# Attention and two MLPs in one program: far weights' conversions counted as ready later, block copies urgent, the first load's gate due sooner

## The chip, the cores and the metric

The kernel runs on one core of a Trainium2 chip. The metric is the device time of one execution in microseconds (us). TensorE multiplies, VectorE, ScalarE and GpSimd do everything between the products, and SyncE (SP) issues all loads and stores. In rows of the profile these are PE (and PEld for its weight loads), DVE, ACT, POOL and SP.

## What is computed

```python
# q, k, v: (2, 8, 576, 64) float32
q_rot, k_rot = rotate(q), rotate(k)                    # rotary positions
scores = q_rot @ k_rot.T / 8
scores = scores - max(scores)
attn = exp(scores); attn = attn / (attn.sum() + 1e-9)
x = attn @ v                                           # -> (1152, 512)
h = maximum(x @ w_in, 0.0)                             # w_in (512, 2048)
y = (h * h) @ w_out                                    # w_out (2048, 512)
out = ((y @ w_a) * (y @ w_b)) @ w2_out                 # (512, 1536) twice, (1536, 512)
```

## The kernel before

**The parts.** The attention part works on eight pairs of heads. A pair has five chunks of scores, (p, 0) to (p, 4), the last a small one. VectorE takes the maximum of a chunk while it moves it out of PSUM (line 440), ScalarE takes the exponent (445), VectorE transposes (462), and TensorE multiplies with V (498), one pair behind. GpSimd rotates q and k of the pair after next (364, 365). Sums of a pair become reciprocals (`recip`, 526: a bias on ScalarE, the reciprocal on VectorE, then `pieces` on GpSimd, which cuts them into three bf16 parts), TensorE turns these (`flip`, 545) and spreads them over the rows (`spread`, 560), and GpSimd scales x (`scale`, 583).

The first MLP has 16 slices of 128 columns. The first four are computed plainly (`unit1`), the others two by two in super blocks (`super1`), and `out1` multiplies with `w_out` in four groups. The second MLP has 12 super blocks (`super2`) for each half of the tokens and sums with `w2_out` (`out2`). A super block makes seven products p1 to p7 of half size instead of eight, with sums and differences of the operands. It keeps partial results in three PSUM banks: after p1, p7 and p6 a copy by ScalarE saves the bank's content (lines 912, 916, 920 in `super2`, 961, 965, 969 in `super1`), and the next product into the same bank is added on top, so p6 waits for p1's copy, p4 for p7's and p5 for p6's.

**Conversion of weights.** The weights arrive as 64-bit floats, 512 KB a slice, and are turned into two float32r parts. `convert` (612) issues the load, then ScalarE scales (622), GpSimd or VectorE clamps (631), VectorE shifts (625) and merges the bits (628). `two_parts` (608) makes the high half on ScalarE and the low half, value less high half, on VectorE or GpSimd (606). For super blocks `prep_pair` adds four sums and differences (689 and after). There are three buffers for raw slices, two each for the scaled ones and for the bits.

**The planner.** The whole order is fixed when the program is built. Each piece of work is an `Op` with the engines that may do it, a cost, its inputs and its buffers. TensorE's order is that in which the ops are written; `order` gives the others a due time, backward from the TensorE op that needs them (`soon` and `anchor` can pull it ahead: due so many us behind the anchor's due time). Then it plays the program through: at each step it takes, over all engines, the op that can start first. On one engine, of the ops that can start first the one due first wins, and only an `urgent` op may be preferred when it can start up to `WAIT` = 0.3 us later. `FLEX` ops, open to VectorE and GpSimd, go to whichever can start them first. The times in the plan are the planner's own; on the chip an engine keeps the planned order and starts each op when its inputs are there.

**Gates and pacing.** Three one-element memsets (1077) stand behind chunks (0, 4), (6, 1) and (6, 3): the loads of the first, second and third weight wait for one each in the plan, later ones for all. `paced` holds the first two weights' scaling back until the exponents of (6, 2) and (7, 2).

Of the kernel before, what the change touches and what calls it, by code (L numbers as in the profile page):

```python
# [74 lines left out]
class Plan:  # L75
# [9 lines left out]

    def op(self, engines, cost, fn, after=(), acq=(), rel=()):
        o = Op((engines,) if isinstance(engines, str) else engines or ("-",), cost, fn, after, acq, rel, len(self.ops))
        self.ops.append(o)
        return o

# [19 lines left out]
        return 0.25 + 2.05 * n  # L110

    RATE = 0.33

    def lasts(self, o, e, s, other):
        took = self.takes(e, o.cost)
# [4 lines left out]
    def order(self):  # L120
# [73 lines left out]
        while True:  # L194
# [5 lines left out]
            for e in engines[1:]:  # L200
                ok = []
                for o in open_[e]:
                    if o.end is None and (r := room(o)) is not None:
                        ok.append((max(at[e], begin(o, e), r), o.due, o.k, o, e))
                first = None
                if ok:
                    near = min(x[0] for x in ok) + self.NEAR
                    x = min((x for x in ok if x[0] <= near + self.WAIT * x[3].urgent), key=lambda x: (0 if e == "SP" else x[1], x[0], x[2]))
                    first = (x[0], x[1], x[3], e)
                if first and (best is None or first[0] < best[0]):  # L210
                    best = first
# [39 lines left out]
def attention_moe_moe2_kernel(ctx: ExitStack, tc: tile.TileContext, qk, rope, vq, ident_in, sel_in, w_in, w_out, w_a, w_b, w2_out, out):  # L251
# [274 lines left out]
    def recip(p):  # L526
        st = ST[p]
        rest = lazy(lambda: st_p.tile([P, 9], F32, tag="rest", name=f"rest{p}"))
        part = lazy(lambda: st_p.tile([P, 27], BF16, tag="part", name=f"part{p}"))
        ex = [x for c in range(5) for x in EXP[p, c][1]]  # L530
        def pieces(e):
            e.tensor_copy(part()[:, 0:9], st()[:, 1, :])
            e.tensor_tensor(out=rest(), in0=st()[:, 1, :], in1=part()[:, 0:9], op=ALU.subtract)
            e.tensor_copy(part()[:, 9:18], rest())
            e.tensor_tensor(out=part()[:, 18:27], in0=rest(), in1=part()[:, 9:18], op=ALU.subtract)

        o = pl.op("ACT", ("us", 0.2), lambda e: e.activation(st()[:, 1, :], st()[:, 1, :], AF.Copy, bias=1e-9), ex)
        o = pl.op("DVE", ("us", 0.14), lambda e: e.reciprocal(st()[:, 1, :], st()[:, 1, :]), [o])
        o = pl.op("POOL", ("us", 1.0), pieces, [o])
        SC[p] = o, part  # L540

    def flip(p, slots, at):
# [108 lines left out]
    count = [0]  # L651
# [7 lines left out]
    def prep_weight(key):  # L659
        if key in W:  # L660
            return
        name = f"{key[0]}{key[1]}"
        b = Buf("bits", tile_of([P, DM], I32, "bits", f"bits_{name}", bufs=2))
        w = slot(name)
        early = count[0] <= EARLY
        o = convert(key, Bits(b), early, count[0] <= MID)
        W[key] = w
        WOK[key] = two_parts(name, DM, lambda: w()[:, 0], lambda: w()[:, 1], lambda: b().bitcast(F32), [o], [b], "POOL" if early else FLEX)
        WOK[key][0].acq.append(w)

    ORDER = {1: (0, 0), 2: (0, 1), 7: (1, 0), 4: (1, 1), 5: (2, 0), 6: (2, 1), 3: (3, 0)}

    def prep_pair(key, ka, kb):
# [2 lines left out]
            return  # L676
        ba = Buf("bits", tile_of([P, DM], I32, "bits", f"bits_p{f}", bufs=2))
        bb = Buf("sums", tile_of([P, 6, 256], I32, "sums", f"sums_{f}"))
        oa = convert(ka, Bits(ba), False)
        ob = convert(kb, Bits(bb, 2), False)  # L680
        w = [slot(f"p{f}_{i}") for i in range(4)]
# [16 lines left out]
        for k, (n, after) in enumerate(((2, [s3, ob]), (2, [s1, s2]), (1, [s4]))):  # L698
# [2 lines left out]
            r[0].acq.append(t)  # L701
            ends += r
        pl.op(None, None, None, ends + [s1, s2, s3, s4], rel=[bb])
        W[key], WOK[key] = w, ok + ends

    def use(key, op):
# [189 lines left out]
    def super2(f, t):  # L896
# [12 lines left out]
        def p1():  # L909
            prep_pair(key, ("a", f), ("b", f))  # L910
            o = prod("al", 1)
            op[1] = pl.op("ACT", ("p", HB), lambda e: e.copy(left(), bk["al"]()), [o], acq=[v])  # L912

        def p7():
            o = prod("be", 7)
            op[7] = pl.op("ACT", ("p", HB), lambda e: e.copy(right(), bk["be"]()), [o, op[1]])

        def p6():
            o = prod("al", 6, [op[1]])
            op[6] = pl.op("ACT", ("p", HB), lambda e: e.copy(u(), bk["al"]()), [o], acq=[u])  # L920

        def p2():
            o = prod("gm", 2)
# [20 lines left out]
    def super1(r, t):  # L944
# [13 lines left out]
        def p1():  # L958
            prep_pair(key, ("i", 2 * r), ("i", 2 * r + 1))
            o = prod("al", 1)  # L960
            op[1] = pl.op("ACT", ("p", HB), lambda e: e.copy(v()[:, lo], bk["al"]()), [o], acq=[v])

        def p7():
            o = prod("be", 7)
            op[7] = pl.op("ACT", ("p", HB), lambda e: e.copy(u()[:, hi], bk["be"]()), [o, op[1]], acq=[u])

        def p6():
            o = prod("al", 6, [op[1]])
            op[6] = pl.op("ACT", ("p", HB), lambda e: e.copy(u()[:, lo], bk["al"]()), [o, op[7]])  # L969

        def p2():
            o = prod("gm", 2)
# [93 lines left out]
    for n, (p, c) in enumerate(order):  # L1066
# [8 lines left out]
        if (p, c) in GATES:  # L1075
            k = GATES.index((p, c))
            wide.append(pl.op("DVE", ("us", 0.06), lambda e, k=k: e.memset(sb.tile([P, DM], I64, tag="raw", bufs=3, name=f"later{k}").bitcast(I32)[:, 0:1], 0), EXP[p, c][1]))
    p = NPAIR - 1
    lasts = [SDONE[6, 4]] + TOK[7]
    pl.op(None, None, None, lasts, rel=[held("g2"), held("g3")])  # L1080
# [150 lines left out]
```

## Time and profile before

| | us |
|---|---|
| median of three runs | 540.14 |
| lowest and highest of them | 538.04, 542.59 |
| the profiled execution | 539.17 |
| its span, first to last instruction | 537.4 |
| TensorE busy in it | 525.0 (98%) |
| VectorE, GpSimd, ScalarE busy | 450.5, 358.0, 306.7 |
| TensorE's granted clock, share of full | 0.999 |

The span is what the rows of the trace lie in; the execution is 1.8 us longer. A busy share is an average over stages, so what a stage can give is read from its own windows and from what TensorE waits for in it. Attention ends near 122 us, the first MLP near 325 us.

### The profile page before, as it was taken

Reading aid. Unit: us, or ns where it says so; the run is one execution under the profiler, and the core shown is the slowest. Engines: PE = TensorE matmul, PEld = TensorE weight load, DVE = VectorE, ACT = ScalarE, POOL = GpSimd, SP = SyncE. Lnnn points to the kernel's source line nnn. Section 1 sums busy time; section 2 is a strip of 40 time slices with the busy share of each in tenths; the row PEclk is TensorE's granted clock in tenths of the full one; section 3 lists DMA queues with packets and bytes.
Section 4 is the critical chain, followed back from the end, with each engine's and each line's share of the span. In section 5 each row is a group of like instructions: output and inputs, shape, how many; then the busy total and the mean of one; then the engine's idle time right before and its main releaser. Section 6 shows DMA issues by size and latency. Waiting matters only on the chain.

```text
span 537.4 us, 13363 instructions
## 1 busy us (share of the span) xinstructions
PE 525.0 (98%) x5390; PEld 473.2 (88%) x5390; DVE 450.5 (84%) x809; ACT 306.7 (57%) x756; POOL 358.0 (67%) x297
## 2 busy tenths in 40 slices
PE   8999999999999899999999998999999999999997
PEld 6666666668999899999999998999999999999996
DVE  5998898897899989889978999898778888788454
ACT  1666888887776685378348645557534444443210
POOL 3875789857899458658636899985578776854000
PEclk9999999999999999999999999999999999999999
DMA  7678777464313413322333202333233223300004
GB/s 231 177 179 179 177 179 183 129 187 142 115 48 114 157 47 112 118 80 79 98 113 105 72 9 78 118 117 121 89 108 113 84 79 117 119 1 0 1 2 176
DMA packets 18914, 58.48 MB, mean 109 GB/s; under 512 B 2313, under 2 KB 4489, under 8 KB 17828
## 3 DMA queue, kind: packets, MB, share of 16 engines
q1 hardware_dynamic: 18852, 57.63, 35.8%
q8 instruction: 42, 0.69, 0.6%
q14 instruction: 20, 0.16, 0.1%
HBM read 55.26 MB, written 2.36 MB: 107 GB/s over the span
## 4 chain that ended last, share of the span: by engine, by line
PE 88%; DVE 7%; issue 1%; DMA 1%; ACT 1%; SPq 0%; POOL 0%; DVEq 0%
PE m L711 13%; PE m L713 13%; PE m L712 13%; PE s L412 8%; PE av L498 8%; PE av L711 6%; PE av L713 6%; PE av L712 6%; PE m L1023 3%; PE m L1024 3%; PE m L1025 3%; PE av L1023 2%; PE av L1024 2%; PE av L1025 2%; PE s L408 1%
## 5 line engine op out<-in xcount | busy, mean ns | idle before, releaser
L445 ACT ACTIVATE PV<-PV,st 128x576 f32<-128x576 f32 x48 | 37.0, 771 | 24.1 <-DVE PV L440 23.7
L364 POOL TENSOR_TENSOR X<-X,cs_rot 128x1152 f32<-128x1152 f32 x14 | 36.9, 2642 | 14.1 <-DMA X<-in_qk 14.0
L440 DVE TENSOR_SCALAR_CACHE_REDUCE PV<-s 128x576 f32<-128x576 f32 x48 | 34.4, 753 | 11.5 <-PE s L412 11.5
L606 POOL TENSOR_TENSOR g<-v,g 128x576 fp32r<-128x576 f32 (+1 forms) x23 | 28.7, 1247 | 20.4 <-ACT g L728 20.4
L631 POOL TENSOR_SCALAR cl_i<-cl_i 128x512 f32<-128x512 f32 x15 | 29.4, 1965 | 7.5 <-ACT cl_i L622 6.5
L713 PE MATMUL m<-g,w_o 128*128 128x384 f32 (+1 forms) x99 | 31.9, 322 | 0.0
L712 PE MATMUL m<-g,w_o 128*128 128x384 f32 (+1 forms) x99 | 31.9, 322 | 0.0
L711 PE MATMUL m<-g,w_o 128*128 128x384 f32 (+1 forms) x99 | 31.9, 322 | 0.0
L728 ACT CAST g<-v 128x576 fp32r<-128x576 f32 (+1 forms) x36 | 21.3, 593 | 18.1 <-DVE v L939 16.7
L764 DVE TENSOR_TENSOR oacc<-m,oacc 128x512 f32<-128x512 f32 (+1 forms) x30 | 20.4, 680 | 13.3 <-PE m L1025 13.1
L498 PE MATMUL av<-PT_acc,PV 32*64 32x160 f32 (+1 forms) x1152 | 25.7, 294 | 2.0 <-issue 2.0
L498 PEld LDWEIGHTS av<-PT_acc,PV 32*64 32x64 f32 x1152 | 19.8, 130 | 7.9 <-issue 6.3
L711 PE MATMUL m<-x,w_b 128*128 128x288 f32 x84 | 24.8, 295 | 1.6 <-ACT v L969 1.6
L412 PE MATMUL s<-cs_rot 64*128 64x288 f32 x128 | 24.4, 434 | 1.4 <-DVE PV L440 0.7
L412 PE MATMUL s<-rot 64*128 64x288 f32 x128 | 24.7, 433 | 1.0 <-DVE bits_i L628 0.7
L498 PE MATMUL av<-PT_wb,PV 32*64 32x160 f32 (+1 forms) x1152 | 25.6, 294 | 0.0
L498 PEld LDWEIGHTS av<-PT_wb,PV 32*64 32x64 f32 x1152 | 19.7, 130 | 6.3 <-issue 4.8
L713 PE MATMUL m<-x,w_b 128*128 128x288 f32 x84 | 24.8, 295 | 0.0
L712 PE MATMUL m<-x,w_b 128*128 128x288 f32 x84 | 24.8, 295 | 0.0
L912 ACT COPY v<-m 128x288 f32<-128x288 f32 x16 | 6.4, 400 | 31.6 <-PE m L713 31.6
L713 PE MATMUL m<-x,w_pp 128*128 128x288 f32 x78 | 23.0, 295 | 0.0
L712 PE MATMUL m<-x,w_pp 128*128 128x288 f32 x78 | 23.0, 295 | 0.0
(324 smaller groups left out, 2156.9 us busy)
## 6 DMA issues: line engine op xcount, KB each, us to landing
PV<-in_vq SPq DMA_DIRECT2D x32, 288.0 KB, 4.5
raw_i<-in_w_in SPq DMA_DIRECT2D x16, 512.0 KB, 3.8
raw_o<-in_w_out SPq DMA_DIRECT2D x16, 512.0 KB, 4.1
X<-in_qk SPq DMA_DIRECT2D x26, 288.0 KB, 5.2
raw_a<-in_w_a SPq DMA_DIRECT2D x12, 512.0 KB, 3.8
raw_b<-in_w_b SPq DMA_DIRECT2D x12, 512.0 KB, 3.7
raw<-in_w_out SPq DMA_DIRECT2D x12, 512.0 KB, 3.7
out<-oacc SPq DMA_DIRECT2D x8, 256.0 KB, 2.0
```

What stands on the lines that cost most here:

```text
L364: m = pl.op(where, ("s", 2 * S), lambda e, qi=qi: e.tensor_tensor(out=x()[:, :, qi, :], in0=x()[:, :, qi, :], in1=cs, op=ALU.mult), [done[ ...
L412: pe.matmul(s[h]()[:, bk, 0:288], q0, k0[h][:, bk * 288:bk * 288 + 288], start=True, stop=True)
L440: m = pl.op("DVE", ("us", 0.7), lambda e, h=h, j=j: e.tensor_scalar(out=PP[pr.k][:, h, :].rearrange("p (b n) -> p b n", b=2), in0=s[h]()[: ...
L445: x = pl.op("ACT", ("us", 0.8), lambda e, h=h, j=j: e.activation(PP[pr.k][:, h, :], PP[pr.k][:, h, :], AF.Exp, bias=st()[:, 0, j:j + 1], s ...
L498: pe.matmul(AV[a]()[half(h), q], v[r, h, b], pt[r, k:k + 4 + both, 32 * b:32 * b + 32], start=(b == 0), stop=(b == KB - 1), skip_group_che ...
L606: e.tensor_tensor(out=out_, in0=a, in1=b, op=ALU.subtract)
L631: e.tensor_scalar(out=dst(), in0=cl(), scalar1=-HI * TURN, scalar2=HI, op0=ALU.max, op1=ALU.min)
L711: pe.matmul(dst, wh, mh, start=first, stop=False, skip_group_check=open_)
L712: pe.matmul(dst, wh, ml, start=False, stop=False, skip_group_check=open_)
L713: pe.matmul(dst, wl, mh, start=False, stop=last, skip_group_check=open_)
L1023: pe.matmul(b(), gt[:, 0, c], w[:, 0, d], start=(k == 0), stop=False)
L1024: pe.matmul(b(), gt[:, 0, c], w[:, 1, d], start=False, stop=False)
```

## The change

Ops made while `pl.far` is set are marked far: those of single weights from the ninth slot on, and all of the pairs. In the choice of the next op, a far op on ScalarE or VectorE that is due more than `AWAY` = 6 us behind its inputs counts as able to start 0.8 us later than its inputs allow (`MARGIN`); an op whose engine or buffer is free later than that is not touched. On GpSimd nothing is added. The six copies behind p1, p7 and p6 become urgent. The pieces of the reciprocals are due 4 us behind their pair's last chunk, the gates' memsets 2.5 us behind their chunk.

```diff
--- before.py
+++ after.py
@@ -85,6 +85,7 @@
 
     def op(self, engines, cost, fn, after=(), acq=(), rel=()):
         o = Op((engines,) if isinstance(engines, str) else engines or ("-",), cost, fn, after, acq, rel, len(self.ops))
+        o.far = self.far
         self.ops.append(o)
         return o
 
@@ -110,6 +111,7 @@
         return 0.25 + 2.05 * n
 
     RATE = 0.33
+    MARGIN, AWAY, far = {"ACT": 0.8, "DVE": 0.8}, 6, False
 
     def lasts(self, o, e, s, other):
         took = self.takes(e, o.cost)
@@ -201,7 +203,8 @@
                 ok = []
                 for o in open_[e]:
                     if o.end is None and (r := room(o)) is not None:
-                        ok.append((max(at[e], begin(o, e), r), o.due, o.k, o, e))
+                        b = begin(o, e)
+                        ok.append((max(at[e], b + (self.MARGIN.get(e, 0) if o.far and o.due > b + self.AWAY else 0), r), o.due, o.k, o, e))
                 first = None
                 if ok:
                     near = min(x[0] for x in ok) + self.NEAR
@@ -537,6 +540,7 @@
         o = pl.op("ACT", ("us", 0.2), lambda e: e.activation(st()[:, 1, :], st()[:, 1, :], AF.Copy, bias=1e-9), ex)
         o = pl.op("DVE", ("us", 0.14), lambda e: e.reciprocal(st()[:, 1, :], st()[:, 1, :]), [o])
         o = pl.op("POOL", ("us", 1.0), pieces, [o])
+        o.soon, o.anchor = 4.0, SDONE[p, 4]
         SC[p] = o, part
 
     def flip(p, slots, at):
@@ -663,10 +667,12 @@
         b = Buf("bits", tile_of([P, DM], I32, "bits", f"bits_{name}", bufs=2))
         w = slot(name)
         early = count[0] <= EARLY
+        pl.far = count[0] > 8
         o = convert(key, Bits(b), early, count[0] <= MID)
         W[key] = w
         WOK[key] = two_parts(name, DM, lambda: w()[:, 0], lambda: w()[:, 1], lambda: b().bitcast(F32), [o], [b], "POOL" if early else FLEX)
         WOK[key][0].acq.append(w)
+        pl.far = False
 
     ORDER = {1: (0, 0), 2: (0, 1), 7: (1, 0), 4: (1, 1), 5: (2, 0), 6: (2, 1), 3: (3, 0)}
 
@@ -676,6 +682,7 @@
             return
         ba = Buf("bits", tile_of([P, DM], I32, "bits", f"bits_p{f}", bufs=2))
         bb = Buf("sums", tile_of([P, 6, 256], I32, "sums", f"sums_{f}"))
+        pl.far = True
         oa = convert(ka, Bits(ba), False)
         ob = convert(kb, Bits(bb, 2), False)
         w = [slot(f"p{f}_{i}") for i in range(4)]
@@ -701,6 +708,7 @@
             r[0].acq.append(t)
             ends += r
         pl.op(None, None, None, ends + [s1, s2, s3, s4], rel=[bb])
+        pl.far = False
         W[key], WOK[key] = w, ok + ends
 
     def use(key, op):
@@ -910,14 +918,17 @@
             prep_pair(key, ("a", f), ("b", f))
             o = prod("al", 1)
             op[1] = pl.op("ACT", ("p", HB), lambda e: e.copy(left(), bk["al"]()), [o], acq=[v])
+            op[1].urgent = True
 
         def p7():
             o = prod("be", 7)
             op[7] = pl.op("ACT", ("p", HB), lambda e: e.copy(right(), bk["be"]()), [o, op[1]])
+            op[7].urgent = True
 
         def p6():
             o = prod("al", 6, [op[1]])
             op[6] = pl.op("ACT", ("p", HB), lambda e: e.copy(u(), bk["al"]()), [o], acq=[u])
+            op[6].urgent = True
 
         def p2():
             o = prod("gm", 2)
@@ -959,14 +970,17 @@
             prep_pair(key, ("i", 2 * r), ("i", 2 * r + 1))
             o = prod("al", 1)
             op[1] = pl.op("ACT", ("p", HB), lambda e: e.copy(v()[:, lo], bk["al"]()), [o], acq=[v])
+            op[1].urgent = True
 
         def p7():
             o = prod("be", 7)
             op[7] = pl.op("ACT", ("p", HB), lambda e: e.copy(u()[:, hi], bk["be"]()), [o, op[1]], acq=[u])
+            op[7].urgent = True
 
         def p6():
             o = prod("al", 6, [op[1]])
             op[6] = pl.op("ACT", ("p", HB), lambda e: e.copy(u()[:, lo], bk["al"]()), [o, op[7]])
+            op[6].urgent = True
 
         def p2():
             o = prod("gm", 2)
@@ -1075,6 +1089,7 @@
         if (p, c) in GATES:
             k = GATES.index((p, c))
             wide.append(pl.op("DVE", ("us", 0.06), lambda e, k=k: e.memset(sb.tile([P, DM], I64, tag="raw", bufs=3, name=f"later{k}").bitcast(I32)[:, 0:1], 0), EXP[p, c][1]))
+            wide[-1].soon, wide[-1].anchor = 2.5, SDONE[p, c]
     p = NPAIR - 1
     lasts = [SDONE[6, 4]] + TOK[7]
     pl.op(None, None, None, lasts, rel=[held("g2"), held("g3")])
```

## Rows read from the trace of the kernel before

**Rows 1.** The page's head and part 1: busy us (share of the span) xinstructions.

```profile
span 537.4 us, 13363 instructions
...
PE 525.0 (98%) x5390; PEld 473.2 (88%) x5390; DVE 450.5 (84%) x809; ACT 306.7 (57%) x756; POOL 358.0 (67%) x297
```

**Rows 2.** Windows: stretch and length, each engine's busy us, clock, DMA share, GB/s.

```profile
29.00:36.00 7.00, 6.73 (x197) 4.78 (x197) 6.85 (x14) 4.61 (x13) 3.60 (x7) 1.00 0.92 228
185.30:303.00 117.70, 117.70 (x799) 117.68 (x800) 101.38 (x204) 74.19 (x180) 75.81 (x63) 1.00 0.28 90
303.00:326.70 23.70, 22.32 (x169) 22.09 (x167) 23.06 (x35) 10.99 (x20) 22.14 (x15) 1.00 0.20 65
326.70:332.20 5.50, 5.04 (x37) 4.81 (x37) 5.47 (x8) 4.76 (x12) 5.50 (x5) 1.00 0.28 105
332.20:516.00 183.80, 183.80 (x1192) 172.47 (x1193) 148.96 (x260) 84.91 (x176) 117.23 (x89) 1.00 0.25 78
```

**Rows 3.** TensorE's waits: line, releaser, us in total, times, longest.

```profile
PE m L711 <- ACT v L969: 1.6, 1, 1.6
PE av L711 <- ACT v L912: 1.4, 1, 1.4
...
PE r L545 <- POOL part L535: 0.5, 2, 0.3
```

**Rows 4.** Timeline near 183 us: start, us, what [idle before <-releaser].

```profile
182.62 0.29 PE L713 MATMUL m<-parts,w_b 128*128 128x288 f32 x1
...
184.28 0.62 ACT L609 CAST w_o<-bits_o 128x512 fp32r<-128x512 f32 x1 [2.38 <-DVE bits_o L628]
...
184.81 0.39 ACT L969 COPY v<-m 128x288 f32<-128x288 f32 x1
...
185.25 0.41 PE L711 MATMUL m<-x,w_b 128*128 128x288 f32 x1 [1.55 <-ACT v L969]
```

**Rows 5.** Timeline near 325 us.

```profile
324.24 0.30 PE L713 MATMUL av<-x,w_b 128*128 128x288 f32 x1
...
325.08 0.62 ACT L609 CAST w_pp<-bits_pp 128x512 fp32r<-128x512 f32 x1 [2.80 <-DVE bits_pp L628]
...
326.32 0.39 ACT L912 COPY v<-av 128x288 f32<-128x288 f32 x1
...
326.77 0.40 PE L711 MATMUL av<-parts,w_b 128*128 128x288 f32 x1 [1.44 <-ACT v L912]
```

**Rows 6.** Timeline near 332 us.

```profile
331.68 0.45 DVE L935 TENSOR_TENSOR v<-av,v 128x288 f32<-128x288 f32 x1
...
332.18 0.40 PE L711 MATMUL av<-x,w_b 128*128 128x288 f32 x1 [0.39 <-DVE v L935]
```

**Rows 7.** Line 606: VectorE's ns min/median/max; GpSimd's busy us, mean ns.

```profile
L606 DVE TENSOR_TENSOR w_pp<-sums_p,w_pp x12: 681/1068/1919, 310.0 to 492.2; 128x512 fp32r<-128x512 f32 x8, 128x256 fp32r<-128x256 f32 x4
...
L606 POOL TENSOR_TENSOR w_pp<-sums_p,w_pp 128x512 fp32r<-128x512 f32 x8 | 11.4, 1419 | 5.4 <-ACT w_pp L609 4.4 <-PE av L713 1.0
```

**Rows 8.** Timeline near 34 us.

```profile
33.14 0.21 DVE L538 RECIPROCAL st<-st 128x9 f32<-128x9 f32 x1
...
34.57 0.23 PE L545 MATMUL r<-small,part 128*27 128x128 bf16 x1 [0.27 <-POOL part L535]
```

**Rows 9.** Timelines of GpSimd, TensorE and SP: a rotation, loads, and their uses.

```profile
29.09 1.42 POOL L365 TENSOR_TENSOR cs_rot<-X 128x576 f32<-128x576 f32 x1
...
35.75 0.51 PE L412 MATMUL s<-cs_rot 64*128 64x288 f32 x2
...
90.34 0.42 SPq L620 DMA_DIRECT2D raw_i<-in_w_in  x1
...
104.50 0.31 SPq L478 DMA_DIRECT2D PV<-in_vq  x1
...
110.55 0.69 PE L498 MATMUL av<-PT_wb,PV 32*64 32x160 f32 x28
```

**Rows 10.** Part 6 of the page: V loads, KB each, median us to landing.

```profile
PV<-in_vq SPq DMA_DIRECT2D x32, 288.0 KB, 4.5
```

## The prediction

> **What bounds the kernel now.** The first view to read is the page's busy times. TensorE is busy 525.0 us of a span of 537.4 us, 98% [rows 1], and the windows of the two long quiet stretches, 185.3 to 303 us and 332.2 to 516 us, have it busy for all of their 117.70 and 183.80 us [rows 2]. VectorE, ScalarE and GpSimd have room in both. So an edit can win only where TensorE stands still, and that is 537.4 - 525.0 = 12.4 us in all, the wait for the first inputs and the last output among it.
>
> The second view is TensorE's list of waits, which says where [rows 3]. Three entries touch this change: 1.6 us, once, for a ScalarE copy at line 969; 1.4 us, once, for the ScalarE copy at line 912; and 0.5 us, in two waits, for GpSimd's pieces of the reciprocals (line 535).
>
> The third view is the timeline around the two large ones, where the reader is to see one pattern twice. In the first [rows 4], TensorE wants the copy that starts at 184.81 us (p6 of a block of the first MLP). The product that it copies ended near 182.9 (the matmul of 182.62 is its last), and ScalarE had been idle from 181.90. But next in ScalarE's order stood the high half of a far weight, `w_o<-bits_o`, and that waited 2.38 us for VectorE's merge. TensorE lost 1.55 us, and 0.41 - 0.29 = 0.12 more in its first matmul behind the stop: 1.67 us. In the second [rows 5], p1's product ended near 324.5 us, ScalarE stood idle for 2.80 us in front of a high half that waited for a merge (325.08), and only behind it came the copy that TensorE wanted (326.32): 1.44 + 0.40 - 0.29 = 1.55 us. Both times the planner had believed the conversion to be ready sooner than it was.
>
> **The change part by part.** Four edits, all to the order that the planner writes; no instruction is added or taken away.
>
> *Ready 0.8 us later, and urgent copies.* In the plan, a far weight's operation on ScalarE or VectorE now counts as ready 0.8 us after its inputs if it is due over 6 us later, and a block's copies p1, p7 and p6 may be preferred when they become ready up to 0.3 us after another candidate. Together, a copy that the plan has ready up to 1.1 us after the high half now goes ahead of it. At 183 us the merge really ended near 184.2, some 1.3 us after the copy could have run. In the plan it came before the copy, by an amount that no trace shows. But ScalarE was free only from 181.90, so a merge planned between 181.8 and the copy's 182.9 is overtaken; I take it that this holds. The copy (0.39 us) then ends near 183.3, before TensorE's stop begins at 185.25 - 1.55 = 183.70, and 1.67 us go. Bounds: 0 if the plan had the merge still earlier, 1.67 if not. The 117.70 us behind have no idle time of TensorE [rows 2], so nothing there takes the gain back. The high half behind the copy comes 0.4 us later, and by the edit's own condition it has over 6 us.
>
> At 325 us the copy may go first in the same way, and 1.55 us go there. What is late next is VectorE: from 326.70 to 332.20 us it is busy 5.47 of 5.50 us [rows 2], and its addition at line 935, which TensorE waits for until 332.18 anyhow, stands in that queue at 331.68 [rows 6]. TensorE that comes 1.55 us sooner waits 1.55 us longer. Bounds: 0 (all given back) to 1.55 + 0.39 + 0.40 - 0.29 = 2.05 us (VectorE's queue gets shorter as well). I take 0.3 us, near the lower end: VectorE's idle time in the 23.70 us before is 23.70 - 23.06 = 0.64 us [rows 2], and half of that could close.
>
> The condition also moves work. GpSimd's candidates are not counted later, so an operation that either engine may do now goes to GpSimd when that one is free within 0.8 us. A low half of 512 columns takes 1.42 us there on average; on VectorE the low halves of that tile take 0.68 us at best and 1.92 at worst [rows 7]. From 332.2 to 516 us GpSimd has 183.80 - 117.23 = 66.6 us to spare [rows 2], so there I take 0; where it has none is a rival below.
>
> VectorE's spread for one kind of operation has a rule beside it. The Trainium skill (Trainium Architecture — The Big Picture, "What this means for kernel authors") says that VectorE and GpSimd contend for a shared port pair by an exclusive lock and not by a split of bandwidth. By that rule work handed to GpSimd would give VectorE nothing back while it runs; the 0.3 us at 325 would be 0 and the whole sum 2.2 us. The spread, a factor of 2.8, agrees with it, though no row shows what GpSimd held at the time.
>
> *Pieces of the reciprocals.* They, and through the planner's backward pass the reciprocal and the bias before them, are now due 4 us after their pair's last score. Before, the first pair's reciprocal ran at 33.14 us, and TensorE's transpose waited for the pieces until 34.57 [rows 8]. One reciprocal of 0.21 us per pair moves ahead of VectorE's transposes, and four small GpSimd operations ahead of a rotation. Gain 0.5 us [rows 3], bounds 0 to 0.5.
>
> *The gates' memsets.* The first one lets the first weight's load go; with a due time 2.5 us behind its scores it moves to the end of the first pair, and the load, whose buffer is still fresh then, goes out there and not at 90.34 us [rows 9]. That is 512 KB more just ahead of the stretch of 29 to 36 us, where the DMA engines are 0.92 busy at 228 GB/s [rows 2]: 2.3 us for what is queued behind it on SP, the V loads and the planes of q and k of the pairs after. Cover: the third pair's rotation ends at 29.09 + 1.42 = 30.51 and TensorE uses it at 35.75, 5.2 us later [rows 9]. Cost 0, and up to 2.3 us if that cover is gone. The conversion itself is held back by pacing until pair 6, so this wins nothing either. The second and third weight's loads move up too, ahead of pair 6's last V loads. Of these the last leaves at 104.50, lands 4.5 us later in the median, at 109.0, and is used at 110.55 [rows 9, 10]: a cover of 1.5 us against 2.3 us, at most 0.8 us lost. I take 0, since the loads would have to meet exactly.
>
> Sum: 1.67 + 0.3 + 0.5 = 2.5 us.
>
> **The rivals.**
>
> *Both stalls stay gone (faster than forecast).* VectorE's stretch from 303 to 332 us gets lighter by two or three operations of 0.68 us that go to GpSimd. For it: VectorE is what TensorE waits for there. Against it: GpSimd is itself busy 22.14 of 23.70 us [rows 2]. It gives 1.67 + 2.05 + 0.5 = 4.2 us.
>
> *The edits change the order but not the end.* The merges were planned over 1.1 us ahead of the copies, or what is won comes back as a wait for the next VectorE operation. The pieces' 0.5 us or nothing is left. For it: the merge was late by some 1.3 us, more than the 0.8 that is added, so all depends on where the plan had the copies.
>
> *GpSimd becomes the bound (slower).* Between 303 and 332 us the new count hands GpSimd far low halves ahead of the splits that the second MLP's products need. Each costs 1.42 us, and GpSimd has 23.70 - 22.14 = 1.56 us left: from the second one on, each delays the splits by 1.42 us. The 2.5 us are gone with (2.5 + 1.56) / 1.42 = 2.9, so three of them; 5.4 us above the time before takes (5.4 + 2.5 + 1.56) / 1.42 = 6.7, seven. For it: GpSimd has hardly any idle time there, and none at all from 326.70 to 332.20 us [rows 2]. Against it: an engine so busy is seldom free within 0.8 us, and then the plan hands it nothing more.
>
> **How the numbers follow.** The profiled execution took 539.17 us for its span of 537.4; the 1.8 us around it stay. 539.17 - 2.5 = 536.7. The median of the three runs, 540.14, lies 0.97 above this execution, so I add that: 537.6 us. Chances: the forecast 0.45 (by itself 536 to 539); both stalls gone 0.22 (540.14 - 4.2 = 535.9); no effect 0.19 (539.6 to 540.1); GpSimd the bound 0.14 (from 540 upward, with half of it above 542). The three runs lie within 4.55 us of each other, so a median of such runs may be off by about a third of that, 1.5 us: 535.9 - 1.5 = 534.4 and 540.1 + 1.5 = 541.6 bound the range, with about a tenth left out on either side. A difference of 1%, 5.4 us, is about what a measurement of this kernel can tell from no change. A gain of that size needs the first rival and a low draw on top, or a wait gone that I have not counted: 0.11. A loss of that size needs seven misplaced operations, half of the last rival: 0.08. Within 1%: 0.81.
>
> **What would show it.** Right: no wait for lines 969 and 912 in TensorE's list, the copy ahead of the high half on ScalarE in both places, a wait for line 935 of about 2 us near 329, the pieces' wait gone, the first weight's load before 30 us and no longer wait for rotations. Wrong: a wait for line 969 of the old size (the plan's lead was larger), TensorE held by a split from GpSimd near 325 us (the slower rival), no wait for line 935 (the first rival), or new waits for V loads near 110 us.

## The result and the profile after

The changed kernel takes 535.12 us in the median of eight runs (533.13 to 538.5), against 540.24 us of eight runs of the kernel before on the same chip: a ratio of 0.9899, with a 95% interval of 0.9875 to 0.9924. The medians lie 5.1 us apart, and the ratio amounts to 5.5 us. The forecast of 537.6 us lay on the right side and the time lies in the range of 534.4 to 541.6, but twice the 2.5 us came. At 1.0% it stands on the bound between faster and same, with a chance of 0.11 given to the one and 0.81 to the other.

The page after the change, whose first lines answer to [rows 1] (busy us, share of the span):

```profile
span 533.4 us, 13367 instructions
...
PE 524.1 (98%) x5390; PEld 473.1 (89%) x5390; DVE 421.1 (79%) x768; ACT 305.1 (57%) x756; POOL 397.4 (74%) x338
```

The span is 4.0 us shorter, as is the profiled execution (539.17 to 535.20 us), with TensorE still at 98%. VectorE went from 450.5 to 421.1 us and GpSimd from 358.0 to 397.4: work did move there as the prediction read it from the missing margin. TensorE's list of waits, the same view as [rows 3]:

```profile
PE av L501 <- issue: 1.2, 1, 1.2
PE av L390 <- POOL small L1077: 1.0, 1, 1.0
PE m L719 <- DVE v L946: 0.9, 1, 0.9
PE s L415 <- DVE cs_rot L379: 0.8, 1, 0.8
PE s L415 <- DVE PV L443: 0.8, 1, 0.8
PE m L719 <- ACT v L925: 0.8, 1, 0.8
PE s L415 <- DVE bits_i L632: 0.7, 1, 0.7
```

Code lines have moved: p1's, p7's and p6's copies are now lines 920, 925 and 930 in the second MLP and 972, 977 and 982 in the first, p5's addition is 946 (it was 935), the reciprocals' last piece 538. The waits for the pieces, for p6's copy and for p1's copy are gone. New are 0.8 us for p7's copy (925), and the wait for p5's addition has grown from 0.4 to 0.9 us.

TensorE runs the same instructions in the same order in both kernels, so each can be compared with itself. The table says how far it comes sooner, worked out from the two traces. A stop without releaser is one for which the profile shows no engine and no load that ended it (`issue` in the list above).

| instruction at, before (us) | sooner by (us) | what lies just ahead of it |
|---|---|---|
| 39.75 | 0.27 | first wait for the pieces is gone |
| 50.11 | 1.51 | a stop without releaser at 48.8 is gone |
| 55.75 | 1.79 | small shifts between |
| 90.75 | 0.23 | a stop without releaser has come at 89.0 (after) |
| 97.50 | 1.49 | the one at 96.2 is gone |
| 104.55 | 1.83 | second wait for the pieces is gone |
| 109.39 | 2.13 | shorter wait for a score eviction |
| 185.25 | 3.81 | p6's copy is no longer waited for |
| 326.77 | 5.39 | p1's copy is no longer waited for |
| 328.46 | 4.54 | p7's copy is |
| 332.18 | 3.87 | p5's addition is |
| the end | 3.97 | |

In the steps of the prediction: pieces 0.27 + 0.34 = 0.6 us (0.5 forecast), p6 1.68 us (1.67), p1's stop 1.58 us won and 0.85 + 0.67 us given back, so 0.06 net (0.3). These are 2.3 us. What the sum did not have is 1.2 us of stops without a releaser and small shifts between them (1.24 + 0.28 - 1.56 + 1.26), and 0.3 us at a score eviction.

The two places in the timeline, columns as in [rows 4] and [rows 5]. ScalarE and TensorE near 181 us after the change:

```profile
179.37 0.62 ACT L613 CAST w_o<-bits_o 128x512 fp32r<-128x512 f32 x1 [0.49 <-DVE bits_o L632]
...
180.85 0.40 ACT L982 COPY v<-m 128x288 f32<-128x288 f32 x1
...
181.44 0.29 PE L719 MATMUL m<-x,w_b 128*128 128x288 f32 x1
...
191.47 0.62 ACT L613 CAST w_o<-bits_o 128x512 fp32r<-128x512 f32 x1
```

The high half at 179.37 is not the one of [rows 4]: it is the one ahead of it, which ran at 180.97 us before. The one that held up p6's copy (184.28 before, the third of its kind from 170 us on in both traces) now runs at 191.47 us, 10 us behind the copy and without a wait, and TensorE goes on at 181.44 with no wait. ScalarE, VectorE and TensorE between 320 and 329 us:

```profile
320.85 0.40 ACT L920 COPY v<-m 128x288 f32<-128x288 f32 x1 [3.79 <-PE m L721]
...
322.41 0.45 DVE L772 TENSOR_TENSOR yacc<-av,yacc 128x288 f32<-128x288 f32 x1
...
322.86 0.29 PE L721 MATMUL av<-x,w_pp 128*128 128x288 f32 x1
322.89 0.67 ACT L613 CAST x<-yacc 128x576 fp32r<-128x576 f32 x1 [1.64 <-DVE yacc L772]
323.47 0.39 ACT L925 COPY v<-m 128x288 f32<-128x288 f32 x1
...
323.92 0.40 PE L719 MATMUL m<-parts,w_b 128*128 128x288 f32 x1 [0.76 <-ACT v L925]
...
326.26 1.62 DVE L610 TENSOR_TENSOR gT<-yacc,gT 128x576 f32<-128x576 f32 x1
...
327.81 0.44 DVE L946 TENSOR_TENSOR v<-m,v 128x288 f32<-128x288 f32 x1
...
328.30 0.40 PE L719 MATMUL m<-x,w_b 128*128 128x288 f32 x1 [0.95 <-DVE v L946]
```

p1's copy (320.85) now runs as soon as its product is done. But the next thing on ScalarE is the high half of a split of y (322.89), which waited 1.64 us for VectorE's late eviction of 322.41, and p7's copy stands behind that. It is the old pattern with another op: the splits are not far, so neither edit touches it. The other half is the one that was forecast: p5's addition at 327.81 stands behind a difference of 1.62 us that VectorE began at 326.26; the one of [rows 6] stood behind a difference of 1.62 us too, begun at 330.13. The windows of the stretch, columns as in [rows 2]:

```profile
181.00:299.00 118.00, 118.00 (x803) 117.84 (x802) 93.42 (x195) 74.04 (x182) 86.88 (x75) 1.00 0.29 94
299.00:322.70 23.70, 23.70 (x181) 23.70 (x180) 22.54 (x33) 9.55 (x17) 21.94 (x15) 1.00 0.13 45
322.70:328.20 5.50, 3.90 (x28) 3.43 (x26) 4.96 (x7) 4.23 (x9) 5.50 (x4) 1.00 0.29 95
```

TensorE now stands still in none of the 23.70 us ahead of 322.7, and for 5.50 - 3.90 = 1.6 us of the 5.50 behind, where it stood 0.46 of 5.50 us before. From 181 to 299 us nothing stops it, as forecast.

### The profile page after: what moved, and what is told of

It reads as the page before. It is cut to its first block, busy times and chain, and to the rows that moved or that the text cites. A ratio compares the mean times of both kernels' runs of the same rounds, so it can differ in the third digit from the quotient of the medians.

```text
span 533.4 us, 13367 instructions
## 1 busy us (share of the span) xinstructions
PE 524.1 (98%) x5390; PEld 473.1 (89%) x5390; DVE 421.1 (79%) x768; ACT 305.1 (57%) x756; POOL 397.4 (74%) x338
## 4 chain that ended last, share of the span: by engine, by line
PE 91%; POOL 3%; DVE 2%; issue 1%; DMA 1%; ACT 0%; SPq 0%; DVEq 0%
PE m L719 13%; PE m L721 13%; PE m L720 13%; PE av L501 9%; PE s L415 8%; PE av L721 6%; PE av L719 6%; PE av L720 6%; PE m L1037 3%; PE m L1038 3%; PE m L1039 3%; PE s L411 2%; PE av L1037 1%; PE av L1038 1%; PE av L1039 1%
## 5 line engine op out<-in xcount | busy, mean ns | idle before, releaser
L610 POOL TENSOR_TENSOR g<-v,g 128x576 fp32r<-128x576 f32 (+1 forms) x26 | 32.0, 1230 | 34.1 <-ACT g L736 34.1
L920 ACT COPY v<-m 128x288 f32<-128x288 f32 x20 | 8.0, 398 | 39.2 <-PE m L721 39.2
L635 POOL TENSOR_SCALAR cl_i<-cl_i 128x512 f32<-128x512 f32 x14 | 27.2, 1949 | 2.1 <-ACT cl_i L626 2.1
L720 PE MATMUL m<-x,w_pp 128*128 128x288 f32 x92 | 27.2, 295 | 0.0
L721 PE MATMUL m<-x,w_pp 128*128 128x288 f32 x92 | 27.2, 295 | 0.0
L719 PE MATMUL m<-x,w_pp 128*128 128x288 f32 x92 | 27.1, 294 | 0.0
L719 PE MATMUL m<-x,w_b 128*128 128x288 f32 x82 | 24.3, 296 | 0.9 <-DVE v L946 0.9
L1037 PE MATMUL m<-w_b,g 128*128 128x512 f32 (+1 forms) x63 | 24.6, 390 | 0.0
```

Of the source, the lines that this page charges most:

```text
L610: e.tensor_tensor(out=out_, in0=a, in1=b, op=ALU.subtract)
L635: e.tensor_scalar(out=dst(), in0=cl(), scalar1=-HI * TURN, scalar2=HI, op0=ALU.max, op1=ALU.min)
L719: pe.matmul(dst, wh, mh, start=first, stop=False, skip_group_check=open_)
L720: pe.matmul(dst, wh, ml, start=False, stop=False, skip_group_check=open_)
L721: pe.matmul(dst, wl, mh, start=False, stop=last, skip_group_check=open_)
L1037: pe.matmul(b(), gt[:, 0, c], w[:, 0, d], start=(k == 0), stop=False)
```

## The experiments

Each ratio is to the kernel before in the same session, with its 95% interval.

**The four edits one by one.** First only the 0.8 us (`MARGIN`, with the marking of far ops):

```diff
-    ok.append((max(at[e], begin(o, e), r), o.due, o.k, o, e))
+    b = begin(o, e)
+    ok.append((max(at[e], b + (self.MARGIN.get(e, 0) if o.far and o.due > b + self.AWAY else 0), r), o.due, o.k, o, e))
```

> Only the 0.8 us are added to far operations; copies are not urgent, pieces and gates as before. My theory: this part alone takes away the ScalarE wait of 1.55 us near 183 us, since in the plan the high half was to start at 172.51 and the copy was ready at 172.94, 0.43 us later, which 0.8 covers without the 0.3; the wait at the second MLP's start goes too and comes back as a wait for a VectorE addition. Time about 1.7 us below before, ratio 0.997 (0.993 to 0.999). Rival (urgency is what does it): the wait for the p6 copy is still in TensorE's list and the ratio is 1.000. Rival (the count's hand-over to GpSimd hurts): ratio above 1.002.

Measured 0.9944 (0.9920 to 0.9969), some 3.0 us. The wait for p6's copy is gone from TensorE's list, and of that for p1's copy (912, here 919) 0.3 us are left:

```profile
PE av L501 <- issue: 1.5, 2, 1.1
PE s L415 <- DVE cs_rot L379: 1.1, 2, 0.6
PE s L415 <- DVE PV L443: 1.0, 2, 0.7
PE av L390 <- POOL small L1070: 1.0, 1, 1.0
PE s L415 <- DVE bits_i L631: 0.7, 1, 0.7
PE r L548 <- POOL part L538: 0.5, 2, 0.3
PE av L718 <- ACT v L919: 0.3, 1, 0.3
```

So the 0.8 us alone remove the two ScalarE waits but for these 0.3 us. In this order nothing near 330 us is given back either: TensorE comes 2.2 us sooner at 185 us and 3.1 at 332, of which 2.7 us are left at 340. The 0.8 us hold on ScalarE and on VectorE, where they also hand work to GpSimd; no run has them on one of the two alone.

Then only the urgent copies:

```diff
+            op[1].urgent = True
```

(and the same for op[7] and op[6], in both kinds of super block)

> Only the six copies are urgent. My theory: 0.3 us is less than the 0.43 us by which the plan had the high half ahead, so the wait of some 1.5 us for the p6 copy near 183 us stays; ratio 0.999 to 1.001. Rival (urgency does it): the wait is gone, ratio 0.997.

Measured 1.0023 (1.0000 to 1.0047). Near 183 us the plan is as the expectation has it, with the far high half ahead of the copy; what remains of that wait is 0.7 us, since the merge comes sooner. The wait for p1's copy (912) is still there, and one for p6's copy in the second MLP (922) has come:

```profile
PE m L711 <- ACT v L912: 1.6, 1, 1.6
PE m L711 <- ACT u L922: 1.1, 1, 1.1
...
PE m L711 <- ACT v L974: 0.7, 1, 0.7
```

Urgency alone is worth nothing, and may cost. The kernel's own plan shows why the 0.8 us do what urgency does not (planner's times, not the chip's; the kernel before):

```
ScalarE  172.51 to 173.13  high half of w_out, its merge ended at 172.41
ScalarE  173.13 to 173.53  copy behind p6, ready at 172.94
TensorE  173.63            p5
```

The copy was ready 0.43 us after the high half could start: more than 0.3, less than 0.8.

Only the pieces:

```diff
+        o.soon, o.anchor = 4.0, SDONE[p, 4]
```

> Only the reciprocals' pieces are due earlier. My theory: TensorE's two waits for the pieces (0.5 us) go, the two large ScalarE waits stay: 0.5 us, ratio 0.999. Rival (the pieces also free TensorE's later attention work, or move the stops without a releaser): 1.5 us or more, ratio 0.997 or less.

Measured 1.0026 (0.9999 to 1.0054): neither theory. The waits for the pieces are gone. The first memset comes at 40.1 us where it was at 96.2, but the second and third come at 110.1 us where they were at 106.5, the loads behind them at 110.2 to 112.2 us (SP), and TensorE waits 0.63 us for a weight of the first MLP at 128 us. The memsets, by their line (1078 here):

```profile
L1078 DVE MEMSET later<- x3: 59/59/59, 40.1 to 110.1; 128x1 int32 x3
```

SP's loads behind them, in the timeline (start, us, engine):

```profile
110.22 0.35 SPq L621 DMA_DIRECT2D raw_i<-in_w_in  x1
...
111.74 0.85 SPq L621 DMA_DIRECT2D raw_i<-in_w_in  x2
```

TensorE's wait for a weight, in the same view:

```profile
128.40 0.44 PE L712 MATMUL m<-x,w_i 128*128 128x384 f32 x1 [0.63 <-ACT w_i L610]
```

In the profile of this kernel p6's wait is longer as well (2.2 us), and behind it the granted clock falls. Windows, columns as in [rows 2], PEclk the third value from the end:

```profile
183.00:187.00 4.00, 2.34 (x17) 2.00 (x15) 3.93 (x7) 2.00 (x4) 1.29 (x1) 1.00 0.44 165
187.00:191.00 4.00, 3.43 (x16) 3.43 (x17) 3.29 (x7) 2.29 (x7) 3.17 (x2) 0.63 0.59 166
191.00:195.00 4.00, 4.00 (x30) 4.00 (x30) 2.70 (x6) 3.27 (x10) 0.61 (x1) 0.94 0.26 100
```

The granted clock of this whole execution is 0.997. Of the twelve executions of this kernel nine have 0.997 or less, of the kernel before 13 of 35; the three others took 540.2 us in the mean, the 22 of the kernel before 540.2. So as far as three executions can tell, what the pieces cost by themselves goes with the clock.

Only the gates:

```diff
+            wide[-1].soon, wide[-1].anchor = 2.5, SDONE[p, c]
```

> Only the gates' memsets are due earlier, so that the first weight's load leaves in the first pair. My theory: no time either way, ratio 0.999 to 1.001, TensorE's waits for ScalarE stay. Rival A (the load at 90 us caused TensorE's stop of 1.0 us without releaser near 96 us, and the gain that the four edits brought beyond my sum came from here): the stop near 96 us is gone and no other takes its place, ratio 0.998. Rival B (the load of 512 KB collides with those of the pairs): POOL's waits for q and k grow by over 2 us and the ratio is above 1.002.

Measured 0.9976 (0.9949 to 1.0002). The stop near 96 us is gone in its profile, but others came near 70 and 90 us; rival B is out, since the ratio is not above 1. With no edit but this the memsets stand at 23.4, 102.6 and 107.8 us.

The parts add up to 0.9944 + 1.0023 + 1.0026 + 0.9976 - 3 = 0.9969, the whole is 0.9899. The difference, 0.0070, is not much more than the five intervals allow together (0.006). That the edits depend on each other is plainer when the gates are left out, below.

**Each edit left out.** The whole change without the urgent copies:

```diff
-            op[1].urgent = True
```

(and the other five lines of this kind)

> The change without the urgent copies. My theory: the 0.8 us alone bring the p6 copy ahead (the copy is planned at 171.89 us, the far operation behind it at 172.29), so TensorE has no wait for a ScalarE copy near 183 us and the ratio is that of the whole change, 0.989 to 0.993. Rival (urgency carries the gain): the wait is back and the ratio is 0.993 to 0.996.

Measured 0.9896 (0.9864 to 0.9927), the same as with them. This is a balance: between 184 and 200 us (times of the kernel before) this version wins 0.7 us less than the whole change, between 324 and 340 us 0.6 us more, since p1's copy holds TensorE up for 0.3 us and neither p7's copy nor p5's addition does. Without the 0.8 us:

```diff
-    MARGIN, AWAY, far = {"ACT": 0.8, "DVE": 0.8}, 6, False
```

(and the marking)

> The change without the 0.8 us. My theory: in the plan the high half (171.30 to 171.92) stands ahead of the p6 copy again, so the waits near 183 and 325 us are back and 1.7 to 3 us are lost against the whole change: ratio 0.994 to 0.998. Rival (the gain lies in the gates and pieces): ratio as with the whole change, 0.990.

Measured 0.9959 (0.9931 to 0.9987). The waits for p1's copy (line 913, 1.6 us) and for p6's copy in the first MLP (line 975, 0.6 us) are back, and 1.1 us for p6's copy in the second (line 923) come as with the urgent copies alone. Without the gates:

```diff
-            wide[-1].soon, wide[-1].anchor = 2.5, SDONE[p, c]
```

> The change without the gates' new due times. In the planner's own account this end is 5.8 us later than with them, in my sum 0 us. My theory: near the whole change, ratio 0.989 to 0.993, the gates cost and win nothing on the chip. Rival (the gates matter once the rest is done, since a late memset shifts the weights behind it): ratio 0.996 or more, with a TensorE wait between 110 and 135 us for a weight.

Measured 1.0047 (1.0017 to 1.0077): slower than before, and the expectation, like the 0 us of the prediction, was wrong. Memsets two and three stand at 109.7 us again, the first three loads of `w_out` slip from 121 to 127 us to 127 to 131 us, and TensorE waits for a weight and then for VectorE:

```profile
PE av L719 <- DVE g L610: 2.0, 1, 2.0
...
PE m L719 <- DVE v L946: 1.4, 2, 0.8
...
PE m L719 <- ACT v L920: 0.9, 1, 0.9
PE m L719 <- ACT w_i L613: 0.8, 1, 0.8
```

Eight of its twelve executions have a clock of 0.997 or less, one of the eight of the whole change. At full clock the two take 540.7 and 534.7 us in the mean.

Without the pieces:

```diff
-        o.soon, o.anchor = 4.0, SDONE[p, 4]
```

> The change without the earlier pieces. My theory: TensorE waits again for the pieces in two transposes (0.5 to 0.6 us), and with the gates early nothing else changes: 0.1% worse than the whole change, ratio 0.990 to 0.992. Rival (the pieces hinder, as they did alone): ratio 0.988 or less.

Measured 0.9953 (0.9921 to 0.9985), worse than the 0.5 us of the pieces explain; two stops without releaser of 1.4 and 1.0 us are in its profile, where the whole change has one of 1.2.

Pieces and gates together, without the other two:

```diff
+        o.soon, o.anchor = 4.0, SDONE[p, 4]
+            wide[-1].soon, wide[-1].anchor = 2.5, SDONE[p, c]
```

> The pieces and the gates together, without the 0.8 us and the urgent copies. Alone they gave ratios of 1.0026 and 0.9976. My theory: together they win more than the sum, since the pieces alone had pushed the second and third memset to 110 us, which the gates undo, and since every look at a kernel with both lacks TensorE's fetch stop at instruction 1473: two waits for the pieces gone (0.6 us), that stop gone (0.6 to 1.7 us), the ScalarE waits of 1.6 and 1.4 us still there; ratio 0.994 to 0.997. Rival (the parts add): ratio 1.000.

Measured 0.9942 (0.9912 to 0.9972), some 3.1 us, where the parts add to 1.0002. So the change is two things of nearly the same worth: the 0.8 us (0.9944) and this pair (0.9942). Their sum, 0.9886, is the whole within its interval, and the urgent copies are worth nothing measurable. The profile of the pair has a stop of 1.8 us without releaser near 90 us and one of 0.7 us in the first MLP.

**What the stops without releaser are.** They stood in TensorE's list before (2.0 us) and were left out of the sum. The instruction queue, by which TensorE's instructions are brought in, has 42 packets of 16,384 bytes in an execution, for the 10,835 instructions in TensorE's rows before (matmuls, weight loads and 55 that wait for semaphores or drain): one for 256 instructions, at 64 bytes each. Every stop without releaser of over 0.3 us, in all profiles, comes right behind the 193rd instruction past a multiple of 256, and just behind a late packet. The one at the 1473rd instruction, near 48 us, read from the packets and instructions of the traces (us):

```
kernel             1217th at   packet          1473rd at   next at
before             44.25       47.42 to 48.64  48.80       50.11
before, once more  44.53       47.58 to 49.09  49.09       50.56
0.8 us alone       44.13       46.71 to 47.88  48.68       49.34
urgent alone       44.13       47.08 to 48.40  48.68       49.86
pieces alone       43.54       46.77 to 47.85  48.20       49.18
gates alone        43.63       46.26 to 47.45  48.19       48.82
without urgent     44.25       46.50 to 47.61  48.97       49.07
without 0.8 us     43.99       46.06 to 47.15  48.54       48.54
without pieces     43.18       46.45 to 47.77  47.73       49.40
without gates      43.76       47.10 to 48.17  48.37       49.67
pieces and gates   43.11       45.37 to 46.48  47.72       47.92
the whole change   44.00       45.83 to 46.91  48.50       48.51
no V loads         43.80       44.88 to 45.97  48.41       48.42
splits far         43.06       45.37 to 46.58  47.67       48.15
```

(The last two kernels come below.)

In every row but that without V loads the next instruction starts 1.3 to 1.6 us behind the packet's end: where the packet comes late against the 1473rd instruction, that is a stop, and where it comes early enough, it is none. The Trainium skill (Runtime: NRT & Kernel Launch, "Instruction fetch mechanics") says that the sequencer refills in 16 KiB blocks of 256 instructions over a DMA queue of its own while it executes, at a cost that is mostly hidden. The blocks agree; in this attention part the cost is not hidden, 0.3 to 1.8 us for one stop.

To see whether loads make the packets late, the change without the V loads of pairs 2 to 7:

```diff
+            if p > 1:
+                LV.setdefault(p, []).append(w)
+                continue
             d = dma(288, lambda e, r=r: e.dma_start(out=V4[r, p % 2], in_=vq[p]), [w])
```

> The change without the V loads of pairs 2 to 7 (24 loads of 288 KB left out, so these pairs multiply with the V of pairs 0 and 1): about half of what the queues carry in the attention part from 40 us on. My theory on TensorE's stops without releaser: they are instruction fetches that come late because the DMA engines are busy with loads; with half the loads none of over 0.3 us is left between 40 and 120 us, and 1 to 2 us are saved: ratio 0.985 to 0.988. Rival (they come by TensorE's own pace of instructions): the stops stay, ratio as with the whole change.

Measured 0.9868 (0.9830 to 0.9906), and in four runs 532.74 to 533.2 us, a spread of 0.5 us where the whole change has 5.4. Its profile has no stop without a releaser. By itself that says little: those without the urgent copies and without the 0.8 us have none of over 0.3 us either, with all loads. The window of 40 to 120 us of this kernel, columns as in [rows 2]:

```profile
40.00:120.00 80.00, 79.58 (x2014) 55.15 (x2001) 74.26 (x146) 67.81 (x219) 64.43 (x65) 1.00 0.22 73
```

The same window of the whole change:

```profile
40.00:120.00 80.00, 78.10 (x2007) 53.89 (x1992) 72.16 (x141) 65.43 (x209) 63.24 (x64) 1.00 0.69 171
```

And of the kernel before, once more:

```profile
40.00:120.00 80.00, 76.58 (x1901) 52.86 (x1902) 69.06 (x141) 62.68 (x200) 58.81 (x65) 0.98 0.67 171
```

The packets say more. At a DMA share of 0.22 the packet of the table leaves 1.1 us behind the 1217th instruction, at 0.65 to 0.70, in the thirteen other profiles, 1.8 to 3.3 us. Over all packets between 40 and 120 us, each taken from the 193rd instruction of its block, it is 0.9 us in the mean and 2.0 at most without the V loads, and 1.8 to 2.6 in the mean and 3.2 to 5.2 at most in the others. So with fewer loads the instructions come sooner, as the theory has it. At which place a packet waits for the loads is not shown.

The kernel before once more:

> The kernel before, looked at once more. My theory: the stops without releaser are again right behind an instruction packet, 193 instructions past a multiple of 256, but not all at the same packets as in the first look (48.80 and 96.21 us); the waits for ScalarE of 1.55 and 1.44 us are the same within 0.1 us. Rival: the same stops at the same places.

540.78 us in one run. The stop at 96 us is not there and one at 91.3 is; the ScalarE waits are 1.6 and 1.4 us again. Behind the stop at 91.3 (1.04 us of idle time) the granted clock falls. Windows:

```profile
89.00:93.00 4.00, 2.96 (x66) 1.74 (x64) 3.20 (x4) 3.38 (x12) 2.40 (x3) 1.00 1.06 233
93.00:97.00 4.00, 4.00 (x60) 2.68 (x59) 1.52 (x5) 0.72 (x2) 3.56 (x4) 0.57 0.88 222
97.00:101.00 4.00, 4.00 (x96) 3.00 (x103) 3.51 (x8) 3.62 (x17) 3.92 (x2) 1.00 0.19 44
```

From 93.07 to 96.48 us TensorE has half its clock, 1.2 GHz, and its lag behind the first profile grows by 1.4 us in that stretch.

**A version beyond the change.** The two waits that are left near 325 us, and 0.7 us at the first weight's merge near 110:

```diff
         def part(i, val, after, frees=()):
+            pl.far = True
             YPART[t][i] = two_parts("", S, lambda: place(t, i, 0), lambda: place(t, i, 1), val, after, list(frees))
+            pl.far = False
...
-            o = pl.op("DVE", ("us", 1.3), lambda e: (shift(e, cl), merge(e)), [o], acq=[up] + bits.acq, rel=[raw_, cl, up])
+            o = pl.op("DVE", ("us", 0.69), lambda e: shift(e, cl), [o], acq=[up], rel=[cl])
+            o.soon, o.anchor = HASTE, SDONE[order[PACE[0] + PACE[1] * turn[0]]]
+            o = pl.op("DVE", ("us", 0.69), merge, [o], acq=bits.acq, rel=[raw_, up])
```

> The change, with two additions: the high and low halves of the splits of y count as far too, and the first weight's shift and merge on VectorE are two operations, so that an eviction may go between. After the change TensorE still waits 0.92 us for p7's copy and 1.1 us for a VectorE addition near 323 to 328 us and 0.8 us near 110 us. My theory: the copy's wait goes, part of the addition's stays since VectorE is the bound there; the 0.8 us become 0.1; in all 1 to 2 us under the change, ratio to before 0.986 to 0.989. Rival (VectorE's queue takes all of it back): ratio as with the change, 0.990.

Measured 0.9907 (0.9875 to 0.9939), no better than the change (0.9899). The wait for p7's copy is gone, and VectorE's addition (line 950 here) takes it back:

```profile
PE m L721 <- DVE v L950: 1.9, 2, 1.0
...
PE av L501 <- issue: 0.9, 2, 0.7
...
PE s L415 <- DVE bits_i L632: 0.7, 1, 0.7
```

1.9 us in two waits, where it was 0.9 us in one. The rival was right, and the 0.7 us near 110 stayed as well. No version that was run and does the whole work beats the changed kernel; the one without urgent copies equals it.

## Why the prediction was right, and where it was short

*p6's copy near 183 us.* Right, in mechanism and size: 1.68 us against 1.67, and the 118 us behind kept it. The assumption about where the plan had the merge, which no trace could show, held: the high half could start 0.43 us ahead of the copy, inside the 0.8. That urgency has a share in it was wrong; the 0.8 us alone do it. The high half was not put 0.4 us later, right behind the copy, but some 10 us behind it.

*p1's copy near 325 us.* Right in the net, 0.06 us against 0.3. VectorE did take it back, but by half: the other half went to a copy behind a split's high half, an op of the same kind that was overlooked because it is not a weight's. With the 0.8 us alone, and with the whole change but for the urgent copies, TensorE had no wait for p7's copy or p5's addition; so this depends on the order that the planner happens to find there, and the urgent copies have a part in it.

*The pieces.* 0.6 us against 0.5, but only in company. With them alone the second and third memset come 3.6 us later, and a wait for a weight has come. The prediction named what the pieces move past on VectorE and GpSimd, and not that the second and third memset could fall back: in the plan of the kernel before they start at 97.4 us and are due at 121.2 and 124.6.

*The gates.* The step that failed. They were taken at 0, with losses as the only bound: the cover of the loads was looked at, the worth of an earlier second and third weight was not. With the rest of the change they are worth the step from 1.0047 to 0.9899, some 8 us, of which 6 are left when only executions at full clock are compared. The third memset comes at 103.6 us for 106.5, the second weight's load at 98.4 for 106.6, the fourth at 111.1 for 113.2. Without the gates the memsets come at 109.7 us and TensorE waits 0.8 us for a weight, which it does not with them: the other edits had made the weights late. What of the rest of the 6 us (2.0 us of waiting for VectorE among it) comes from late weights is not shown. The first weight's load did leave at 22.85 us in place of 90.34 with no harm to the rotations, as forecast.

*Stops without a releaser.* 2.0 us of them stood in the list of waits and were not made a term. The pair of pieces and gates takes one away: in every profile of a kernel without the pair (the two of the kernel before among them) the 1473rd instruction's packet comes late and TensorE stops for 0.6 to 1.7 us, in every one with it and all V loads it stops for under 0.5 us. The packet then leaves 1.8 to 2.3 us behind the 1217th instruction, and without the pair 2.6 to 3.3 us. Why is not settled: it was not tried which load it waits behind.

*From the execution to the median.* The 0.97 us between the profiled execution and the median were carried over as if they belonged to both kernels. After, the profiled execution lies 0.08 us above its median. The executions differ by such stops and by the clock behind them, which the change alters, so part of the gain in the medians (5.1 us, where the profiles show 4.0) lies there. The granted clock of each execution tells a part of it: 0.997 or less in 38 of 92 executions of the kernel before, in the four sessions of the experiments, and in one of eight of the whole change. The 54 at full clock took 539.9 us in the mean, the 38 others 542.2, and the seven at full clock of the whole change 534.7. So at full clock the change gives 5.2 us, from all executions 5.7; about 0.5 us is the clock. The kernels ran in different sessions, so this is rough.

*The range.* That the median lies in it is in part luck. Its lower end was set by the rival in which both stalls stay gone, and that did not come: the terms of the sum gave 2.3 us, as forecast, and the rest came from the stops, a score eviction and the clock, for which the sum had nothing. The prediction had this case in one clause, a wait gone that was not counted.

*GpSimd the bound.* It did not come. GpSimd is busy 21.94 of 23.70 us ahead of 322.7, about as before, and what was handed to it went to stretches with room: from 181 to 299 us it is busy 86.88 us, where it was 75.81 in the stretch before. The exclusive lock between VectorE and GpSimd, which the prediction weighed from the Trainium skill (Trainium Architecture — The Big Picture, "What this means for kernel authors"), did not keep VectorE's busy time from falling by 29 us while GpSimd's rose by 39. No run separates what the lock cost.

## What to carry to other kernels

In a planned order an engine stands still behind an op whose input comes later than the plan had it; a small margin on ops that are not needed soon is cheap and moved both large waits here, while a preference for the urgent op won nothing: its window of 0.3 us was shorter than the 0.43 us by which the plan had the other op ahead. An edit that moves ops ahead moves others back: look for those with late due times, and test edits together as well as alone. A stop that the profile gives no releaser is a term too: see whether it comes at a fixed count of instructions, and how busy the DMA engines are there.

## What the hardware showed that was not expected

TensorE's instruction fetch is often late in the attention part, where 256 instructions last about 5 us and the DMA share is 0.65 to 0.70: none to four stops of 0.3 to 1.8 us in a profiled execution, at different blocks from one to the next, and in one of them (pieces and gates) a stop of 0.7 us in the first MLP too. With a DMA share of 0.22 there is none, and the runs lie within 0.5 us of each other.

After some stops the granted clock fell to 1.2 GHz: for 3.41 us behind a stop of 2.2 us (pieces alone), for 3.41 us behind one of 1.04 us (the kernel before, once more) and for 6.83 us behind one of 1.3 us (gates alone). Behind the stops of 1.55 us at 183 us it did not fall in either profile of the kernel before, nor behind the stop of 1.8 us at 90 us (pieces and gates). So the size of the one stop does not decide it; what does the runs do not show.
